# A fused attention and long-convolution kernel: one list of turns, engines and buffer slots exchanged for another

## The chip, the cores and the metric

The kernel runs on one core of a Trainium2 chip. The core has a matrix engine (TensorE, PE in the profile), a vector engine (VectorE, DVE), an activation engine (ScalarE, ACT), a general engine (GpSimd, POOL) and a sequencer that issues transfers (SyncE, SP); sixteen DMA engines move the data. Each engine works through its own list of instructions in order and waits on semaphores for the others. The metric is the time on the device in microseconds (us), the median of several executions.

## What is computed

Two independent parts stand side by side in the output. Part A is attention with a memory over segments: 2048 positions of 576 channels, 32 heads of 18 channels, four segments of 512 positions. Part B is a gated convolution: a short filter of four taps on k, a product with v, a causal convolution over the whole sequence with a filter of 2048 taps for each channel, and a product with q.

```
# part A, for each of four segments s
p     = softmax(q_s k_s^T * scale + mask)        # mask: -1e9 where row < column
a_dot = p v_s
a_mem = (phi(q_s) M) / (phi(q_s) z + 1e-6)
o     = g * a_mem + (1 - g) * a_dot
M    += phi(k_s)^T v_s ;  z += sum phi(k_s)
out_A = concat(o) @ wo
# part B
k_shift = 4-tap causal filter of k ;  kv = k_shift * v
y       = irfft(rfft(kv padded) * rfft(ssm_k padded))[:S] + kv * ssm_D
out_B   = q * y
out     = concat([out_A, out_B], axis=-1)
```

## The kernel before, in words

The program first builds a graph of 1317 operations (`Prog.build`), each of them a few instructions with the buffers it reads and writes. Nothing in the kernel decides an order at run time: three tables of numbers, `TURN`, `ENGINE` and `SLOT`, say in which order the operations are written out, on which engine each of them stands where two are possible, and which copy of a rotating buffer each logical buffer takes. `plan()` reads them, and the loop `for o in order: o.fn(o.eng)` writes the instructions. The order on an engine is therefore that of `TURN`, and all transfers are issued by SyncE in that order, one behind the other: a transfer whose data is not ready holds up all that stand behind it.

```
    order, eng, slot = ints(TURN, "H"), ints(ENGINE, "B"), ints(SLOT, "B")
    for b, k in zip(bufs, slot, strict=True):
        b.slot = k
    return pr, [ops[i] for i in order]
```

The names used below, with the lines of their instructions:

- Part A, segment s (0 to 3): the transposing loads of x, five tiles `xT` (L737, "x1" is segment 1); the products with wq and wk on TensorE (L136, out in PSUM), their casts to `dn` (L142 on ScalarE, L144 on VectorE), the stores of `dn` to a scratch in memory (L768, "qd") and the padded loads of four heads from it (L778, "pad s.hg"). For each group of four heads, 32 groups in all (numbered 0 to 31): scores on TensorE (L966, "s0", "s1", "s2"), exps on ScalarE (L973, two of 128x1024 for each score block), masks on GpSimd (L980), the product with V (L138, "av"), its copy `ou` and the store of it to a second scratch (L1026, "ad"). From that scratch the sums (L1040, "cs") and the numerators (L1068, "am") of a segment are read back, divided (L1046, L1047, L1074), joined with the memory part (L1083, and L804, L810 for phi) and multiplied with wo ("out", L136); the output leaves at L1104 ("oA").
- Part B, five groups of channels (0 to 4, the last one half as wide): the transposing loads of k (L389, "kT") and v (L392, "vT"), the four-tap filter as products with diagonal matrices (L136, "conv") and the product with v on VectorE (L422), the store of it (L428, "kvst"). The long convolution is a chain of small products: "F1" (L138, reads `xs`, loaded at L455 as xsh from the filter or xsx from kv; 512 KB), "F2", products on VectorE (L525 and following), "inv" into `Z`, a transposing transfer of `Z` to `CT` (L558, "zt"), "last" (L138, reads `CT`), the product with q (L585) and the store (L592, "yo").
- Constants: tables of sines on ScalarE (L274, L276, L322), which need the sine set of ScalarE's function tables, while L643, L804 and L973 need the exp set; copies and casts need neither. An ACT_TABLE_LOAD stands wherever the set changes.

Buffers rotate over few copies: five tiles `xT` (so x of the next segment waits until the last product with this segment's x is done), three `pad`, four `X` for k and v, one `Z` and one `CT`.

Of the kernel before, what the change touches and what calls it, by code (L numbers as in the profile page):

```python
# [1159 lines left out]

ENGS = ("PE", "ACT", "DVE", "POOL", "SP")
TURN = (
    "AwBqAAAAVABnAFUAAgABAGgAawBpAFMACABWAAQAbwBZAGwAHABXAGQAWABtAHAAWgBbAGYAngAFAGMAnQCaAAkACgALAG4ADACbAHEAZQCfAB8AiQAeAIwAIQAgAA0AmAB7AIgAlwCcAA4AHQB8AI"
    "sAoQCNAJkAIgClAA8ABwCKAKAAdQB2AKYAowCBACMApAAQAHcAeQBeAKIAeACRACQAkgCTAHoAJQCAACYAlQB+AKkAJwCqAJQAsAAoALIAlgAZACkADwQsAKsAfwCxAHIArAARAF8AtAAaACoAtQBz"
    "ABAEtgC4ABcEdAARBLkAjgC6ABUEYQCzAI8APQEYBBMEPgEUAIIAFgQSBBUAtwAUBJAAuwC8ABcAvQA7ARIAPAETAD8BGACnAKgAGQQiBCoEvwAjBMEAKwQtAK0AwAB7AcMAKwB6AcQArgB8ARYAMg"
    "QzBMIAxQBAAcoAQQHLABoEQgHMAMYAIARcASEEGwTHAB4EvgAfBMgAfQAuAM4AXQHPAC8AMgDQAEsEMAAcBB0EgwDSAF4BhAAxAGAB1AAkBNMAMwBEAdkAQwHRACUE2gAmBBsAXwGFAE8BYADJAM0A"
    "3QDbAEwERQHVAN8A3gCYATQAUAHWACcEYgHkAJkBNQDXAOYAKATlANwA6AApBOAA4QDpADoE6gDiADsELAQdAS0E7ADuAGUBNARGAS4ENQTnAGMBLwRkAUcB2ABIAeMAVQTtAPcAMATrADYEZgH4AD"
    "EEIAH5AO8AGAFnAfAASgHxAPMA9ABoAUkBNwRRBGEBhgBNBEsB9QBTBFIENwBPBE4EVARDBDwE+gD2AIcAUAT7APwAPQQZAWkBcQE4BDkAOQRiAAIBHAFqAR8BawEeAUQENgAEATgAUQFcAGwBVQEh"
    "Af0ABgFtAQMBCAHyAAcBOwA6ADwAPgQNAa8AcgEPAQ4BbwFdAAUBPwRNAUwBPQD+AP8AQAQ+AE4BQQQAAREBEwFzAQkBEAFcBIcEWASaAVMBXQQSAZsBAQFZBAoBtAFUAQsBnAG2AZ0BUgEUAVYEbg"
    "FBAEIEtQEVAXcBgQGAAXABFgF+AX0BQAAGAD8AVwQXAXgBeQG3AYIBdQGtAYMBdAF/Aa8BdgGEAa4BDAGgAYUBNQKwAVoEngGhAaUBhgFbBIcBNgKfAaYBQgCnAagBNwKpAUMARQAjARoBRACrAUYA"  # L1170
    "qgG4AboBrAFHBEcAOAIbAUUEsQEpAbkBRgQoAWAEsgFhBCIBuwGIAVcBJgEqASUBJAFWAUgAJwG8AWgEvQFYAaIBSARpBMcByQE0AcgBiQGPATkCMwFLADUBowGKAbMBvwHKAYsBwAGQATABNgGRBM"
    "EBLwGMAb4BkQHOAdABXgQxAW4EXwRvBGYElQHPAUkAdgRnBHUCKwF3BGoELAF0AmIELQHSAWsEYwRsBMIB1AF2Ao0B0QFkBG0EWQHTAcMBiASOAZYBxAFlBMUB1QHWAUoAlwGSAVAAxgFNANcBLgHY"
    "Ad0BTABPAE4A3wHLAd4BcATMAVEAcQSTAZQBOwLZAc0BeATbAToC2gF5BDwCDQI+AkkE4QFaAuAB3AFyBHoEPQJzBFYCPwLiARICdATjAQ4CWQJ7BFcCNwHkAewBdQRYAloB7gFKAhECOAFbAeUB7Q"
    "FdAkkCOQFcAuYBEwIWApICkwJbAvMBFQJ8BF4C7wH1AUoEjwT0AYsEfQRfAhcClAKQBGAClQJDAugBRAKMBOoB6QHrAWECRQJ+BGsC+wFoAv0BRgLwAfwB8QH3AfYBRwKNBGwC+QH4AecBbQJ/BGkC"
    "TAKJBI4ESAJvAvIBlgSKBEEC+gGXBG4CcAICAkACAwL+AZoCagIEAv8BBgKABJsCQgIAAsMEYgKYApkCgwQFAmUCGgJjAggCkgRPAgcCmAROAgkCcQJkAoEEkwTEBHIClASCBJkEUAJzAgoClgKVBJ"
    "cCdwILAmYCeAJ5AoQEpwJnAn4CAQKpAlIAqAJ7AnoCpAE6AUsCfAIMAqMCGAJ9AoACfwKGBKoCpQKfAh4CIgKkAqECoAKcAg8CnASBAp0EpASaBDIDnQIvA6YCMwObBKICogSrAqMEpQSuAhACsAId"
    "AqwCrwKqBBkCMQOrBBsCHwIhArECMAMUArIEggIjAiACxQSzBJ4EHAJRAjQDsgLGBJ8ENQO0ArMCwQKtAsMCMgFNAiQCwgK1Ai0CLgI2A8QCLwKPArkCtgKQAlEDUwIlAoYCQwMwAiYCugKmBIUEuw"
    "K9ArcChwKRAr8CJwKgBIgCyAJSAr4CKgLJAoMCoQQpAsoCzAK4ArwCKwLNAsACywJQA8UChAKMAs4CNwPNBMYChQLXAo0CiQLZAtgCUgNVAo4COAPbAjkDzwLcAtACOwPdAscC0wKKAtECiwJUAzoD"
    "DAPVAtQC5gLeAtICVAI8A9oCaAPoAqcEaQPiAucC5AJEAywCagPWAgcD4wLfAuACqATpAu0C7wLlAjEC4QJTA6kEMgIIAw8D7gIQA6wECwOtBLQEMwJXA/ACRQNVAw0DrgTqAusCVgM+A7UE9QIRA/"
    "YCtgT3Aj0DtwTxAhIDuATzAuwCPwO8BK8EuwTyAlgDAANIAwEDsAT4ArkE/AL0AgID+QJJA7EEQQP9Av4C+gKBA4MDAwNAA/8CfQNCA4IDBAP7AmMDWgOeAmIDXANZA38DYAMFAxQDXQNmA34DZQNe"  # L1180
    "A18DDgNkA1sDZwOMA44DawMoAmEDkAONA5IDugQGA70EkQNsAxgDCQPLBL4EvwQKA8cEzATABMkEyATQBG0DygQcAzQC0QTUBEoD0gTTBBsD1QQXA84EbgMZA4ADEwNxA5MD1gQdAxUDzwTeBIUD1w"
    "TCBN8EFgMeAxoD2ASGAycDKAOEAyMDRwP/BCQDhwMpA4gD2QRyA28D2gTBBIkDJQNzA4oDSwObA3ADKgMmA0wD2wR6A5wDjwOdA+AEdwOUA9wERgOVA90ElgOqA+EE6ASrA+YEKwPpBOIEiwMsA6wD"
    "5wR7A3gDnwP4BOMEfAMtA6ADeQMfA6ED6gTrBCADpgOoA60DpwPkBCEDogOXA5gDAAXwBHQDmQPlBJ4DqQOaA+4ErgPvBK8D8QS1A6MDdQPyBKQDdgO2A+wD7ARNA7cDAQXtBMAD8wTBA7gDAgX3BP"
    "QEBQWwA8IDxAPGA6UDCAXFAwMF9QQJBQYFuQPDA+UDBAUKBfADugPHA7sDBwW8AwwF5gMWBRQFDQULBesD7QPvA/EDFQXIAxcFsQPuA8kDGAX2BE4DTwP5BLID+wSzA7QDywPKAxkF+gT8BL0DvgPN"
    "A8wD0wPVAyIDGgUOBQ8F3gPUA98DGwUSBf0E2gMTBf4E4AO/AxAF3APnA+ED1gPbA88DIAXOAy4D0APRAxEFHwUcBd0DHQXiA/QD0gPXA/ID6APjA+QD8wPYA9kDHgX1AyEF9gPpA/wD6gMiBfcD+A"
    "MkBfkD+wP6A/0D/gMABP8DAQQCBAQEAwQHBAUEBgQIBAwECQQLBA0EIwUKBA4E")
# [81 lines left out]
```

## Time and profile before

| | |
|---|---|
| median of 3 runs | 342.2 us (341.65 to 343.16) |
| the profiled execution | 346.51 us, its span 344.8 us |
| busy over the span | PE 270.6 us (78%), ACT 247.3 (72%), DVE 244.9 (71%), POOL 105.8 (31%) |
| DMA, queue of SyncE | 51.99 MB in 132142 packets, 71.7% of sixteen engines' time |
| mean granted clock of TensorE | 0.931 |

The span is the time from the first to the last instruction; 1.7 us lie around it. No engine is busy all the time. Busy shares are averages over the whole program: what sets the pace is read for each stretch by itself, from which wait ends last there.

### The profile page before, as it was taken

What the parts mean: (1) busy time and instruction counts of PE and PEld (TensorE: products, weight loads), DVE (VectorE), ACT (ScalarE), POOL (GpSimd) and SP (SyncE); (2) the same over time, 40 slices, a digit from 0 to 9 for tenths busy, and PEclk for the clock granted to TensorE, in tenths of its full rate; (3) what the DMA queues carried; (4) which work ended last, traced back from release to release, by engine and by line L of the source; (5) the groups of instructions that cost most, each with busy time, mean ns of one, the idle gap of its engine ahead of it and who ended that gap; (6) DMA issues with size and microseconds to landing.
All of it is one profiled execution on the core that took longest, in us unless ns stands there. A gap on an engine that the chain in (4) does not pass through costs nothing.

```text
span 344.8 us, 9276 instructions
## 1 busy us (share of the span) xinstructions
PE 270.6 (78%) x3850; PEld 167.3 (49%) x3855; DVE 244.9 (71%) x400; ACT 247.3 (72%) x290; POOL 105.8 (31%) x150
## 2 busy tenths in 40 slices
...
GB/s 138 279 115 155 191 130 155 196 110 163 193 182 195 188 153 212 155 205 60 164 192 130 248 92 163 197 171 92 135 165 132 130 165 120 95 177 80 139 57 84
DMA packets 132184, 52.58 MB, mean 152 GB/s; under 512 B 112430, under 2 KB 124910, under 8 KB 132142
## 3 DMA queue, kind: packets, MB, share of 16 engines
q1 hardware_dynamic: 132142, 51.99, 71.7%
...
## 4 chain that ended last, share of the span: by engine, by line
PE 30%; DMA 20%; ACT 18%; DVE 15%; SPq 12%; issue 5%; POOL 0%; DVEq 0%; ACTq 0%
PE PS L136 18%; ACT P L973 14%; PE PS L138 8%; DMA am<-a_scratch 5%; SPq L737 5%; DMA pad<-qk_scratch 5%; PE PS L966 3%; DMA CT<-Z 3%; DMA a_scratch<-ou 2%; DMA X<-in_B_v_dram 2%; DMA skb<-in_B_shift_k_dram 2%; DVE am L1074 2%; DVE dn L144 1%; ACT A L142 1%; DVE xs L315 1%
## 5 line engine op out<-in xcount | busy, mean ns | idle before, releaser
L973 ACT ACTIVATE P<-PS 128x1024 bf16<-128x1024 f32 x160 | 154.2, 1035 | 43.6 <-PE PS L966 33.4
L980 POOL TENSOR_SCALAR_AFFINE_SELECT P<-P 128x512 bf16<-128x512 bf16 (+1 forms) x112 | 79.5, 725 | 199.1 <-ACT P L973 116.8
L966 PE MATMUL PS<-pad 18*128 18x128 bf16 (+3 forms) x512 | 35.9, 314 | 12.5 <-DMA pad<-qk_scratch 5.7
L136 PE MATMUL PS<-xT,wq 128*126 128x512 bf16 (+1 forms) x100 | 28.4, 415 | 11.6 <-DMA xT<-in_A_x_dram 11.1
L966 PEld LDWEIGHTS <-pad 18*128 18x128 bf16 x512 | 11.2, 93 | 36.2 <-issue 26.8
L136 PE MATMUL PS<-wo,am 126*128 126x288 bf16 (+1 forms) x160 | 26.7, 322 | 2.4 <-DVE am L1083 1.1
L136 PE MATMUL PS<-X,dg 128*128 128x512 bf16 x75 | 21.6, 416 | 7.6 <-DMA X<-in_B_k_dram 6.3
L138 PE MATMUL PS<-P,V 128*32 128x256 bf16 (+3 forms) x512 | 23.8, 307 | 4.4 <-ACT P L973 1.6
L136 PE MATMUL PS<-xT,wk 128*126 128x512 bf16 (+1 forms) x100 | 26.6, 400 | 0.5 <-DMA wk<-in_A_wk_dram 0.4
L144 DVE CAST dn<-PS 126x1024 bf16<-126x1024 f32 (+1 forms) x16 | 19.5, 1219 | 9.4 <-ACT P L973 4.4
L138 PE MATMUL PS<-G,PQ 64*128 64x128 bf16 (+1 forms) x640 | 23.5, 225 | 3.3 <-ACT P L973 1.7
L138 PEld LDWEIGHTS <-Ft 128*64 128x64 bf16 x704 | 21.2, 114 | 7.2 <-issue 6.4
L138 PEld LDWEIGHTS <-PQ 64*128 64x128 bf16 (+1 forms) x640 | 20.5, 102 | 8.4 <-issue 7.0
L136 PE MATMUL PS<-wv,xT 128*128 128x288 bf16 x160 | 22.6, 291 | 2.2 <-ACT V L142 1.5
L138 PE MATMUL PS<-A,Ft 128*64 128x128 bf16 (+1 forms) x640 | 22.6, 223 | 2.0 <-ACT P L973 1.0
L138 PE MATMUL PS<-W,xs 128*64 128x128 bf16 x576 | 20.9, 220 | 4.1 <-ACT P L973 2.3
L136 PEld LDWEIGHTS <-wq 128*126 128x126 bf16 (+1 forms) x100 | 13.3, 141 | 21.2 <-issue 9.4
L144 DVE CAST A<-PS 128x1024 bf16<-128x1024 f32 x18 | 21.6, 1217 | 2.7 <-PE PS L138 2.6
L422 DVE TENSOR_TENSOR X<-PS,X 128x1024 bf16<-128x1024 f32 x10 | 12.1, 1222 | 15.7 <-PE PS L136 14.2
L138 PEld LDWEIGHTS <-xs 128*64 128x64 bf16 x576 | 17.9, 109 | 9.0 <-issue 7.8
L136 PEld LDWEIGHTS <-am 126*128 126x128 bf16 (+1 forms) x160 | 16.8, 109 | 11.2 <-issue 3.0
L804 ACT ACTIVATE fe<-dn 126x512 bf16<-126x512 bf16 (+1 forms) x30 | 19.1, 639 | 2.4 <-DVE fk L810 1.9
...
## 6 DMA issues: line engine op xcount, KB each, us to landing
...
```

The costliest lines, as they stand in the source:

```text
L136: self.nc.tensor.matmul(out, lhsT=lhsT, rhs=rhs, start=start, stop=stop)
L138: self.nc.tensor.matmul(out, lhsT=lhsT, rhs=rhs, start=start, stop=stop, tile_position=pos)
L142: self.nc.scalar.copy(out=out, in_=in_)
L144: self.nc.vector.tensor_copy(out=out, in_=in_)
L315: v.tensor_scalar(out=self.i32(ix), in0=self.i32(it), scalar1=self.t(self.bcol)[:, 0:1], scalar2=self.t(off)[:, 0:1], op0=ALU.mult, op1=AL ...
L422: self.nc.vector.tensor_tensor(out=self.t(kv)[:, sl], in0=self.psf(pc), in1=self.t(vT)[:, sl], op=ALU.mult)
L737: self.nc.sync.dma_start_transpose(out=self.t(b)[:], in_=self.A_x[0, L * s:L * s + L, c0:c0 + P])
L804: self.nc.scalar.activation(out=self.t(fe)[0:M], in_=self.t(dense[m])[0:M, w_, :], func=ACT.Exp)
L966: nc.tensor.matmul(o, lhsT=t[r, 1, q0:q0 + P], rhs=t[r, 0, q0:L], start=True, stop=True, tile_position=(32 * j, 0))
L973: self.nc.scalar.activation(out=out2(jj), in_=self.psf(pso[jj]), func=ACT.Exp, scale=scale)
L980: self.nc.gpsimd.affine_select(out=ap, in_=ap, compare_op=ALU.is_ge, fill=0.0, base=0, pattern=pat + [[1, P]], channel_multiplier=-1)
L1074: self.nc.vector.tensor_tensor(out=self.t(b)[0:M], in0=self.psf(pR)[0:M], in1=self.t(b)[0:M], op=ALU.mult)
```

## The change

Only the three tables are different. The operations, their instructions, shapes and buffers are the same; the turns are others on every engine and in the transfer queue, and some casts and evictions that either ScalarE or VectorE can do, and some sums that VectorE or GpSimd can do, stand on the other engine (ScalarE has 283 operations instead of 282, VectorE 308 instead of 309). The diff is three long strings; the first line of each:

```
 TURN = (
-    "AwBqAAAAVABnAFUAAgABAGgAawBpAFMACABWAAQAbwBZAGwAHABXAGQAWABtAHAAWgBbAGYAngAFAGMAnQCaAAkACgALAG4ADACbAHEAZQCfAB8AiQAeAIwAIQAgAA0AmAB7AIgAlwCcAA4AHQB8AI"
...
+    "AwBoAFYAAABrAAEAWAACABwACABXAFMAagBpAGcAVQBUAAQAHgAdAG0ABQAJAAoAWwAfAGwAbwBuAAsAcABxAGQAWQCJABQAWgCIAIsAZQAMAA0AXgBmABUAEgCMABMADgAgAJcAigCNAHsAmACaAJ"
...
```

Three places of the new order follow. The first is SyncE's queue in the first third, around the first transfer of `Z` to `CT` (zt0). The names are X4 for the rotating k and v tiles, qk_scratch and a_scratch for the two scratches. Before:

```order
L428 DMA kv_scratch_171<-X4_0_99 128x2048
L455 DMA xs_1_104<-in_B_ssm_k_dram 128x32x64
L768 DMA qk_scratch_172<-dn_1_120 4x18x1024
L778 DMA pad_2_130<-qk_scratch_172 128x1024
L768 DMA qk_scratch_172<-dn_0_119 7x18x1024
L558 DMA_TRANSPOSE CT_0_98<-Z_0_101 128x32x128
L392 DMA_TRANSPOSE X4_1_100<-in_B_v_dram 128x2048
L389 DMA_TRANSPOSE X4_0_99<-in_B_k_dram 128x2048
L1026 DMA a_scratch_173<-ou_1_158 128x512
```

Now:

```order
L455 DMA xs_1_104<-kv_scratch_171 128x32x64
L392 DMA_TRANSPOSE X4_1_100<-in_B_v_dram 128x2048
L778 DMA pad_0_128<-qk_scratch_172 128x1024
L778 DMA pad_2_130<-qk_scratch_172 128x1024
L428 DMA kv_scratch_171<-X4_0_99 128x2048
L558 DMA_TRANSPOSE CT_0_98<-Z_0_101 128x32x128
L1026 DMA a_scratch_173<-ou_1_158 128x512
L1026 DMA a_scratch_173<-ou_0_157 128x512
L389 DMA_TRANSPOSE X4_0_99<-in_B_k_dram 128x2048
```

The load of the third filter group (xs from in_B_ssm_k) and two stores to qk_scratch are gone from between the store of kv and zt0; the load of v stands ahead of zt0, that of k two rows behind it.

The second place is ScalarE at the start. W1, psc and Ft are the sine tables, fe an exp of phi, gg two exps of the gate, G and dn and V and phk casts, P4 the exps of the scores. Before:

```order
L804 ACT_TABLE_LOAD
L804 ACTIVATE fe_1_166<-dn_0_119 126x512
L804 ACTIVATE fe_0_165<-dn_1_120 126x512
L142 CAST V_1_132<-PS_63 128x32x18
L322 ACT_TABLE_LOAD
L322 ACTIVATE Ft_79<-xs_0_103 128x16x64
L142 CAST dn_0_119<-PS_63 126x1024
L142 CAST V_3_134<-PS_63 128x32x18
L804 ACT_TABLE_LOAD
L804 ACTIVATE fe_0_165<-dn_0_119 126x512
```

Now:

```order
L804 ACT_TABLE_LOAD
L804 ACTIVATE fe_1_166<-dn_1_120 126x512
L322 ACT_TABLE_LOAD
L322 ACTIVATE Ft_79<-xs_0_103 128x16x64
L142 CAST G_80<-PS_63 128x1024
L804 ACT_TABLE_LOAD
L804 ACTIVATE fe_0_165<-dn_0_119 126x512
L142 CAST G_80<-PS_63 128x1024
L322 ACT_TABLE_LOAD
L322 ACTIVATE Ft_79<-xs_0_103 128x16x64
```

The sines and the exps alternate oftener: the whole list of ScalarE has 8 ACT_TABLE_LOAD where it had 6, all of them in the first part. The loads of x for segment 1 wait on the last product of segment 0 that reads x; it is the 29th operation of TensorE's list before and the 32nd now.

The third place is SyncE's queue near the end, where the transfer of Z for the fourth group (zt3) and the last pads stand. Before:

```order
L1040 DMA cs_0_167<-a_scratch_173 64x1x128
L1068 DMA am_5_147<-a_scratch_173 126x1x512
L558 DMA_TRANSPOSE CT_0_98<-Z_0_101 128x32x128
L778 DMA pad_2_130<-qk_scratch_172 128x1024
L778 DMA pad_1_129<-qk_scratch_172 128x1024
L1026 DMA a_scratch_173<-ou_0_157 128x512
```

Now:

```order
L778 DMA pad_1_129<-qk_scratch_172 128x1024
L1026 DMA a_scratch_173<-ou_1_158 128x512
L778 DMA pad_2_130<-qk_scratch_172 128x1024
L558 DMA_TRANSPOSE CT_0_98<-Z_0_101 128x32x64
L1040 DMA cs_1_168<-a_scratch_173 64x1x128
L1026 DMA a_scratch_173<-ou_0_157 128x512
```

zt3 stands 16 rows ahead of the second pad now and no longer right before the two; the transfer in the last fence is the fifth one (zt4), half as large, which stood between the last stores of ou (L1026) and the last sums (L1040) before.

## Rows read from the trace of the kernel before

**Rows 1.** Busy time by stretch: start:end, length, then each engine, clock, DMA, GB/s.
```profile
0.00:45.00 45.00, 28.40 (x190) 15.95 (x192) 26.65 (x60) 24.85 (x31) 18.51 (x30) 0.96 0.81 174
98.00:130.00 32.00, 22.55 (x274) 12.73 (x274) 20.53 (x38) 18.27 (x23) 7.47 (x10) 0.89 0.93 184
255.00:300.00 45.00, 35.51 (x716) 25.38 (x713) 35.08 (x46) 35.54 (x41) 14.16 (x19) 0.92 0.58 131
300.00:322.00 22.00, 16.37 (x335) 10.94 (x327) 13.98 (x20) 17.89 (x21) 6.63 (x9) 0.77 0.59 136
322.00:345.00 23.00, 10.10 (x52) 5.97 (x52) 6.47 (x10) 2.30 (x4) 0.00 (x0) 0.70 0.35 84
```

**Rows 2.** Waits of PE from 45 to 345 us: total, times, longest.
```profile
PE PS L138 <- DMA CT<-Z: 10.1, 2, 7.4
PE PS L136 <- DMA X<-in_B_k_dram: 6.3, 1, 6.3
PE PS L136 <- DMA xT<-in_A_x_dram: 1.8, 1, 1.8
```

**Rows 3.** Timeline of PE, 97 to 131 us: start, length, engine, line, instruction.
```profile
115.67 1.29 PE L136 MATMUL PS<-fq,zm 126*128 126x128 bf16 x20
123.25 0.59 PE L136 MATMUL PS<-X,dg 128*128 128x512 bf16 x1 [6.28 <-DMA X<-in_B_k_dram]
```

**Rows 4.** Timeline of SyncE's queue (SPq), 100 to 131 us.
```profile
102.47 0.34 SPq L428 DMA_DIRECT2D kv_scratch<-X  x1
102.85 0.42 SPq L455 DMA_DIRECT2D xs<-in_B_ssm_k_dram  x1
103.60 3.16 SPq L768 DMA_DIRECT2D qk_scratch<-dn  x1
...
107.31 1.34 SPq L768 DMA_DIRECT2D qk_scratch<-dn  x1
108.76 7.32 SPq L558 DMA_TRANSPOSE CT<-Z  x1
116.12 2.68 SPq L392 DMA_TRANSPOSE X<-in_B_v_dram  x1
118.89 2.21 SPq L389 DMA_TRANSPOSE X<-in_B_k_dram  x1
```

**Rows 5.** Issues of the transposes of Z: ns min/median/max, first and last start.
```profile
L558 SPq DMA_TRANSPOSE CT<-Z x5: 3084/5356/7315, 108.8 to 323.7; - x5
```

**Rows 6.** The same for the stores to qk_scratch (L768).
```profile
L768 SPq DMA_DIRECT2D qk_scratch<-dn x20: 666/775/3157, 18.7 to 276.5; - x20
```

**Rows 7.** Timeline of ACT, 30 to 46 us.
```profile
36.23 1.94 ACT L973 ACTIVATE P<-PS 128x1024 bf16<-128x1024 f32 x2 [0.48 <-PE PS L966]
38.18 1.28 ACT L322 ACT_TABLE_LOAD   x1
39.48 1.06 ACT L322 ACTIVATE Ft<-xs 128x1024 bf16<-128x1024 int32 x1
```

**Rows 8.** Timeline of SyncE's queue, 295 to 345 us.
```profile
298.05 5.36 SPq L558 DMA_TRANSPOSE CT<-Z  x1
303.51 0.98 SPq L778 DMA_DIRECT2D pad<-qk_scratch  x2
...
311.76 1.32 SPq L1026 DMA_DIRECT2D a_scratch<-ou  x1
316.60 0.74 SPq L1040 DMA_DIRECT2D cs<-a_scratch  x1
...
321.92 1.69 SPq L1026 DMA_DIRECT2D a_scratch<-ou  x2
323.65 3.08 SPq L558 DMA_TRANSPOSE CT<-Z  x1
326.85 1.24 SPq L1040 DMA_DIRECT2D cs<-a_scratch  x1
```

**Rows 9.** Timeline of ACT, 290 to 345 us.
```profile
309.35 3.77 ACT L973 ACTIVATE P<-PS 128x1024 bf16<-128x1024 f32 x4 [3.26 <-PE PS L966]
313.83 5.80 ACT L973 ACTIVATE P<-PS 128x1024 bf16<-128x1024 f32 x6 [0.71 <-PE PS L966]
319.49 1.92 ACT L142 CAST Z<-PS 64x1024 bf16<-64x1024 f32 x2
```

More of the change, by code (lines that the diff above doesn't have):

```diff
@@ new lines @@
+    "AwBoAFYAAABrAAEAWAACABwACABXAFMAagBpAGcAVQBUAAQAHgAdAG0ABQAJAAoAWwAfAGwAbwBuAAsAcABxAGQAWQCJABQAWgCIAIsAZQAMAA0AXgBmABUAEgCMABMADgAgAJcAigCNAHsAmACaAJ"
+    "sADwCdAJwAEACeABYApQCfAF8AIwB2AKYAmQB1ABEAfAAhAIAAdwAPBCIAcgCjAJIAcwCkALAAdACOAJEAoQCyAH0AoACTALEABwCiAI8AqQB+ABAEqgAZAJAAgQAXABoApwC0ALMAqAC1ABgAEwQR"
+    "BCUAFAQkABIEtgCCAHkAYwC3ACYAeABcALgAegA7ASgAPQEVBLoAFgS5ABcEYgAnADwBYACVABgElAC/ACkAwQC7AMAAvADDAJYAxADCAKsAvQCsACIEPwEjBMUArQA+AYMAygCuACoEKwQyBMYAyw"
+    "DMADoExwB9ASoAyAAzBDsEzgB/AAYAvgDNAF0A0AB+AX8BzwBAASsA0gBBAdQAQgHZABkE0wDaAF8BQwHVANsA3QCFAN8ARAHRAC0A3gCEABwERQFcAckAhgAaBNwAHgQgBBsEHQRgAR8E1gAhBOAA"
@@ new lines @@
+    "FQUfA20DDQUgAyEDjwOTA5sDnQMrA/YELAOcA54DlwOUAw4FLQNuA5gDcQMPBZ8DlQOZA28DcANyA4sD+wShA5oDIgP5BKADcwMuA6ID+gRNAxAFJwMRBUwD/AQoA6YDowMpAyQDdwN0A5YDpAMjA/"
+    "4EdQN2A6cD/QSoA6oDeAMlAxIFqwN5A6wDsQMWBRMFsgOpA7MDFwUYBbkDrQO7A3oDrgO6A7UDewO0A7cDGQWvA3wDtgOlAxwFwAPCA08DGgW8A8EDHQUbBbADxAPFA7gDxgO9A74DwwNOA8cDHgXP"
+    "A9oD0QPIA9sD0APlA9wD3QPTA9UD0gPJA78D1APLA9YD5gPsA80DygPMA94DJgPgA+sDHwXOAyAF7QPnA+8DKgPoA/AD1wPfA/ED8gPhA+ID2APuAyEF8wMiBfQD2QPjA+QD9QPpA/gD/APqA/YD+w"
+    "P9A/cD/gP5A/oDAAT/AwQEIwUBBAMEAgQFBAYEJAUHBAgEDAQLBAkECgQNBA4E")
```

81 lines of the change are left out of this document (37 added, 44 removed).

## The prediction

> **What bounds the kernel now.** I read the shares by engine first, then the busy time by stretch, the waits of TensorE, the timelines around the longest waits, and SyncE's queue there. The shares say that no engine bounds the whole: TensorE, ScalarE and VectorE are each busy for 71 to 78% of the span. By stretch [rows 1] TensorE is idle for 45 - 28.40 = 16.6 us of the first 45, for 9.45 us from 98 to 130, for 9.5 us from 255 to 300, 5.6 from 300 to 322 and 12.9 in the last 23. These five stretches hold 54 us of its idle time; between them it is nearly full and its own work sets the pace. So what the order of turns can change is what TensorE waits for in these five, and whether new waits appear between them.
>
> Its waits name transfers [rows 2]: 10.1 us for `CT`, the transposed Z, in two waits of 7.4 and 2.7; 6.3 us in one wait for k; 1.8 us for x. The one for k stands behind the 20 products of the memory's denominator, which end at 116.96, and lasts to 123.25 [rows 3]. Why k is late is read from SyncE's queue [rows 4]: the store of kv at 102.47, the load of the third filter group (xs, 512 KB), two stores to qk_scratch, then zt0, whose issue alone takes 7.32 us, then v, and k as the last at 118.89. The issue of a transfer lengthens when those ahead of it are not drained: a store to qk_scratch takes 3.16 us there, its median is 0.775 [rows 6]; zt0 takes 7.32, the median of the five is 5.356 [rows 5].
>
> At the end zt3 takes 5.36 us and the last two pads stand behind it [rows 8], and ScalarE then waits 3.26 us for the scores that need them [rows 9]. After the last exps (at 319.49 ScalarE goes over to Z) come the last stores of ou, zt4, the last sums, and the tail to 344.8.
>
> **The change part by part.** The sum is made against the profiled execution, 346.51 us with 344.8 us of span; the median of the runs shown is 342.2, so a time on its scale is multiplied by 342.2/346.51 = 0.9876 for the forecast.
>
> *The start: +3.0.* ScalarE gets two table loads more, of 1.28 us each [rows 7]: 2.57 us. They stand in its list ahead of the first exps, so nothing on ScalarE itself hides them; what can hide them is that it is idle for 45 - 24.85 = 20.15 us of that stretch anyway [rows 1], which gives a lower end of 0. The loads of x for segment 1 and all that stands behind them in SyncE's queue wait for a product that is three operations later; if that delay adds to the loads once more, the upper end is twice 2.57, or +5.1. I take 3.0, the loads and a little of the second, since the loads are the row nearest.
>
> A rule of the Trainium skill speaks against this part: "ScalarE: Activation LUTs", section "What ACT_TABLE_LOAD costs", puts a switch of the function set at about 2.66 us, the load and a drain of 1.38 us. The trace does not bear out the drain: a pair of exps starts at 36.23 and takes 1.94, the load starts at 38.18, and the sine at 39.48 [rows 7], so the switch is 1.30 us in all. By the rule the two switches would cost 5.3 us and the sum would be 2.7 us later, 341.1 us on the median's scale.
>
> *The wait for k: -5.0.* Between the store of kv and zt0 the load of xs and the two stores are gone [the order, first place]. What they cost is read as the excess over the medians behind xs: 3.16 - 0.775 = 2.4 us on the first store, 1.34 - 0.775 = 0.6 on the second, 7.32 - 5.36 = 2.0 on zt0, and the medians of the two stores and 0.42 of xs itself, 2.0 us; together 7.0 us [rows 4 to 6]. Two things take some of it back: two stores of ou stand between zt0 and k, and v stands ahead of zt0 now, where it must wait until the four-tap filter of the third group has left its buffer. I allow 2 us for both, the length of v's 2.68 less a part of it that is covered by TensorE's own work. That leaves 5.0. The ends are -6.3, the whole wait, and 0, if zt0 itself, which still stands ahead of k, is what keeps k late.
>
> *zt3 away from the last pads: -2.8.* The pads are no longer behind its 5.36 us; the wait of ScalarE for the scores is 3.26 [rows 9]. Most of it goes. Next late is TensorE's own work for these scores, which costs the rest. Ends: -3.3 and 0.
>
> *The tail: -1.0.* zt4 (3.08) leaves the place between the last stores of ou and the last sums. But the sums read what these stores write: with the store issued at 311.76, the sums came at 316.60, 4.84 us later; with the stores of 321.92 they came at 326.85, 4.93 later [rows 8]. So zt4 lies beside the landing and hides nearly whole. What goes is the longer issue of the sums behind it, 1.24 against 0.74, and the two casts of Z (1.92, of which the masks behind the last exps cover the greater part) [rows 8, 9]. Ends: -2.5 and 0.
>
> *New waits between the stretches: +2.0.* Three transposing loads now stand in SyncE's queue right behind a store that needs a late result: k of the fifth group behind a store of ou, two of the five x of segment 3 behind a store of oA, and zt2 behind another store of oA. I price them at one wait like that for x, 1.8 us [rows 2]. Ends: 0, and 6.3, a wait like that for k.
>
> All other moves I cost at nothing: the same instructions are covered by the same neighbours where TensorE is full. Where a move takes the cover away, it shows as a wait of TensorE of about 0.5 us, as there are many now.
>
> Sum: +3.0 - 5.0 - 2.8 - 1.0 + 2.0 = -3.8 us. 346.51 - 3.8 = 342.7, times 0.9876 is 338.4 us.
>
> **The rivals.** *A denser end (faster).* From 255 to 322 ScalarE is idle for 9.46 + 4.11 = 13.6 us [rows 1]. The change puts the convolution's work of the fourth group well ahead of this place, so that exps are left with little else between them. If ScalarE is idle for only 5 us there, this term is -8.6 in place of -2.8: -9.6 in all, 336.9, or 332.7 us. For it: exps that follow each other take 0.97 each without a gap [rows 7, 9]. Against it: their scores still wait for pads, and the clock granted to TensorE is 0.92 and 0.77 there [rows 1], lower when it has less to do.
>
> *k is late as before (no change).* zt0 still stands ahead of k. If its 7.32 us are the transpose's own and not the backlog's, the term for k is 0: +3.0 + 0 - 2.8 - 1.0 + 2.0 = +1.2, 347.7, or 343.4 us. For it: other zt's take 5 us and more with less ahead of them [rows 5]. Against it: the store ahead of it was slow too [rows 4].
>
> *The queue's head waits (slower).* The three loads behind late stores: SyncE stands still until an eviction is done, and x, k and `CT` come late one after the other. At 3.4 us each, between the 2.7 of the shorter wait for `CT` and the 6.3 for k [rows 2], they cost 10.2 in place of 2.0: +4.4 in all, 350.9, or 346.5 us. It decides the sign from 5.8 us of such waits on. For it: SyncE's queue is what TensorE's longest waits go back to now. Against it: TensorE has other work in its list between the store's source and the load's user.
>
> *A switch of table sets at twice its load*, by the gaps on ScalarE, would give 341.1 us; the rows show none such, and I count it in with no change at 0.02.
>
> **How the numbers follow.** Forecast 0.40, denser end 0.18, k late as before 0.15 (with the 0.02), the queue's head 0.27. The time is that of the forecast, 338.4 us; its own range, with the ends of the terms taken half, is 335 to 342. The range of 8 in 10 reaches half way past the two outer cases: 330.5 to 347. A measurement of this kernel can tell about 0.5%, 1.7 us, from no change. Faster than 340.5: 0.37 of the forecast's 0.40 and the denser end, 0.55; slower than 343.9: 0.27 for the queue's head; the rest, 0.18, is the same.
>
> **What would show it.** Right: the first exps come no more than 3 us later than 36.2; eight table loads of 1.28 us; TensorE's wait for k is under 2 us; ScalarE has no gap of 3 us in its last 40 us; no single wait for x, k or `CT` above 2.5 us in the middle. Wrong: the first scores of the next groups fall 5 us and more behind, k still ends a wait of 5 us, or new waits for `CT`, x or k stand between 130 and 260 us. If ScalarE's last exps follow without gaps from some 280 us on, the end is denser than I take it.

## The result and the profile after

The changed kernel takes 333.84 us (median of 4, 329.13 to 337.65) beside 342.68 us for the kernel before (341.65 to 343.94) on the same chip; the ratio is 0.9659, with a 95% interval of 0.9546 to 0.9772. It is taken over undisturbed executions alone and so lies below the ratio of the two medians, 0.974. On another chip it took 334.63 beside 343.88. It is faster by some 9 us, where 3.8 were forecast: the sign and the range of 330.5 to 347 held, but the forecast's own range of 335 to 342 did not, the size was more than twice the forecast, and the rival called the denser end, 332.7 us, came closer.

The profiled execution took 334.69 us with a span of 333.0, against 346.51 and 344.8: 11.8 us of span less. The profiled execution of the kernel before is longer than its median by 3.8 us, so differences between these two traces come out somewhat larger than those of the medians. The busy time by stretch of the changed kernel (columns as in [rows 1], the last two stretches cut at the end of its last exp):

```profile
0.00:45.00 45.00, 25.27 (x213) 16.32 (x214) 20.56 (x57) 29.60 (x35) 12.40 (x26) 0.96 0.72 168
45.00:98.00 53.00, 46.26 (x682) 27.10 (x681) 46.65 (x74) 44.48 (x54) 25.05 (x33) 1.00 0.92 173
98.00:130.00 32.00, 26.66 (x343) 15.97 (x342) 21.03 (x37) 22.93 (x29) 7.24 (x10) 0.89 0.83 170
130.00:200.00 70.00, 61.44 (x914) 39.54 (x911) 61.03 (x97) 52.40 (x64) 15.94 (x21) 0.98 0.85 170
200.00:256.00 56.00, 51.23 (x845) 33.25 (x841) 45.64 (x70) 50.69 (x56) 20.10 (x27) 1.00 0.69 156
256.00:310.10 54.10, 43.05 (x791) 27.45 (x795) 38.35 (x55) 48.51 (x54) 23.27 (x31) 0.93 0.64 148
```

The kernel before in the stretches that [rows 1] does not have in this cut:

```profile
45.00:98.00 53.00, 46.40 (x742) 28.29 (x739) 44.24 (x73) 43.02 (x51) 16.02 (x27) 0.97 0.89 156
130.00:200.00 70.00, 63.02 (x942) 40.10 (x942) 59.00 (x100) 56.67 (x68) 18.68 (x27) 1.00 0.75 168
200.00:256.00 56.00, 49.26 (x653) 28.79 (x647) 39.66 (x60) 49.43 (x58) 24.31 (x30) 0.97 0.67 147
256.00:319.70 63.70, 49.11 (x989) 34.34 (x990) 47.66 (x64) 50.45 (x58) 19.55 (x26) 0.87 0.57 130
```

ScalarE does all the exps, so its last exp is a good place to cut: before it ends at 313.83 + 5.80 = 319.63 us [rows 9], now at 310.05. Up to there ScalarE is busy for 248.61 us instead of 242.69 (+5.9, of which two more table loads are 2.6), and idle (length less the fourth engine's figure) by so much less or more: -4.75 in the first 45 us (its busy time there is 4.75 longer), -1.5 to 98, -4.7 to 130, +4.3 to 200, -1.3 to 256, and -7.7 from there to the last exp (63.70 - 50.45 = 13.25 before, 54.10 - 48.51 = 5.59 now). Together -15.5 + 5.9 = -9.6. The rest comes behind the last exp: 344.8 - 319.63 = 25.2 us before, 333.0 - 310.05 = 22.95 now, -2.2. What the stretch of k gives (-4.7) is given back in the next one (+4.3); what stays is the end. Counted by exps it is the same: in the traces the 111th of the 160 starts at 244.7 us, 11 us later than before (233.7), the 141st at 291.3 beside 291.5, the last at 308.9 instead of 318.6. The new order puts exps off, does work of the convolution in their place, and gains among the last twenty.

The waits of TensorE from 45 us on (total, times, longest), to be laid beside [rows 2]:

```profile
PE PS L138 <- ACT P L973: 6.2, 17, 0.6
PE PS L136 <- DVE rs L1047: 5.7, 3, 3.7
PE PS L966 <- DMA pad<-qk_scratch: 4.2, 1, 4.2
...
PE PS L136 <- DMA X<-in_B_k_dram: 0.6, 1, 0.6
```

The kernel before has two more waits among its first four, which [rows 2] does not show:

```profile
PE PS L138 <- ACT P L973: 8.5, 18, 2.3
PE PS L966 <- DMA pad<-qk_scratch: 5.7, 4, 2.6
```

The waits for `CT` and for x are gone, that for k is 0.6. What leads now, short waits for exps, is not new. Pads were waited for before as well, four times; the one wait of 4.2 us that is left is explained by SyncE's queue (start, length, line, transfer):

```profile
99.54 5.81 SPq L392 DMA_TRANSPOSE X<-in_B_v_dram  x1
105.39 1.72 SPq L778 DMA_DIRECT2D pad<-qk_scratch  x2
107.21 0.38 SPq L428 DMA_DIRECT2D kv_scratch<-X  x1
107.69 6.27 SPq L558 DMA_TRANSPOSE CT<-Z  x1
...
115.16 2.36 SPq L389 DMA_TRANSPOSE X<-in_B_k_dram  x1
```

k is issued only 3.7 us earlier than in [rows 4], behind a zt0 that still takes 6.27. TensorE no longer waits for it because other products stand in its list first: its products with k begin at 124.55. The price of having v ahead is the late pads. It follows the length of v's issue, which differs from execution to execution of the same order: 5.81 us and a wait of 4.2 here, 3.63 and 2.0 in the second profile below, 2.34 and no wait in the run with four exps twice.

At the end, ScalarE (start, length, instruction and count, wait before it):

```profile
289.50 7.44 ACT L973 ACTIVATE P<-PS 128x1024 bf16<-128x1024 f32 x8
297.11 12.94 ACT L973 ACTIVATE P<-PS 128x1024 bf16<-128x1024 f32 x14 [0.17 <-PE PS L966]
```

Twenty-two exps follow each other in 20.55 us with one wait of 0.17 us, where [rows 9] has 3.26 and 0.71 among its last ten. In the kernel before the last twenty-two take 31.3 us, from 288.33 on, and the waits are the smaller part of that: eight casts of ScalarE stand between them, 7.8 us, six of them the convolution's. Three lines of them (`A`, `Hx` and `PQ` are the fifth group's):

```profile
297.93 1.10 ACT L142 CAST A<-PS 128x1024 bf16<-128x1024 f32 x1
...
300.66 2.03 ACT L142 CAST Hx<-PS 128x1024 bf16<-128x1024 f32 x2
302.56 1.05 ACT L142 CAST PQ<-PS 128x1024 bf16<-128x1024 f32 x1
```

Now none stands there: six of the eight are done by VectorE, two earlier on ScalarE. And the tail of the queue:

```profile
299.42 3.04 SPq L558 DMA_TRANSPOSE CT<-Z  x1
...
311.95 1.94 SPq L1026 DMA_DIRECT2D a_scratch<-ou  x2
...
315.49 0.69 SPq L1040 DMA_DIRECT2D cs<-a_scratch  x1
```

zt4 is 16 us ahead of the last sums, which come 3.54 us after the start of the stores that they read, instead of 4.93.

The granted clock is not the cause. A second profile of the changed kernel (span 332.4) has nearly the mean granted clock of the kernel before, 0.933 beside 0.931, and TensorE as long busy as before, 270.6 us; the first line of its page's busy times:

```profile
PE 270.5 (81%) x3855; PEld 168.6 (51%) x3855; DVE 240.8 (72%) x399; ACT 252.4 (76%) x293; POOL 105.4 (32%) x150
```

Its idle time is 332.4 - 270.5 = 61.9 us, against 344.8 - 270.6 = 74.2 before.

### The profile page after: what moved, and what is told of

The parts are those of the page before. It is cut to its first block, busy times and chain, and to the rows that moved or that the text cites. A ratio compares the mean times of both kernels' runs of the same rounds, so it can differ in the third digit from the quotient of the medians.

```text
span 333.0 us, 9289 instructions
## 1 busy us (share of the span) xinstructions
PE 265.6 (80%) x3855; PEld 166.7 (50%) x3855; DVE 241.5 (73%) x399; ACT 252.3 (76%) x293; POOL 105.2 (32%) x150
## 4 chain that ended last, share of the span: by engine, by line
PE 37%; ACT 21%; DVE 17%; DMA 15%; issue 5%; SPq 4%; POOL 0%; DVEq 0%; ACTq 0%
PE PS L136 20%; PE PS L138 13%; ACT P L973 13%; DMA a_scratch<-ou 5%; PE PS L966 4%; DMA am<-a_scratch 3%; DMA cs<-a_scratch 2%; DMA X<-in_B_v_dram 2%; SPq L737 2%; DVE Hx L144 2%; DVE A L144 2%; DVE dn L144 1%; DVE PQ L525 1%; DMA wq<-in_A_wq_dram 1%; DVE am L1074 1%
## 5 line engine op out<-in xcount | busy, mean ns | idle before, releaser
L973 ACT ACTIVATE P<-PS 128x1024 bf16<-128x1024 f32 x160 | 153.3, 1033 | 25.3 <-PE PS L966 17.2
L980 POOL TENSOR_SCALAR_AFFINE_SELECT P<-P 128x512 bf16<-128x512 bf16 (+1 forms) x112 | 81.1, 740 | 187.6 <-ACT P L973 147.1
L966 PEld LDWEIGHTS <-pad 18*128 18x128 bf16 x512 | 11.8, 93 | 37.6 <-issue 29.7
L138 PE MATMUL PS<-P,V 128*32 128x256 bf16 (+3 forms) x512 | 25.2, 322 | 5.1 <-ACT P L973 3.0
L136 PE MATMUL PS<-xT,wq 128*126 128x512 bf16 (+1 forms) x100 | 26.0, 399 | 1.9 <-ACT P L973 1.2
L136 PE MATMUL PS<-wo,am 126*128 126x288 bf16 (+1 forms) x160 | 24.5, 307 | 3.7 <-DVE am L1083 2.0
L136 PE MATMUL PS<-wv,xT 128*128 128x288 bf16 x160 | 24.1, 304 | 2.7 <-ACT phk L142 2.0
L136 PEld LDWEIGHTS <-wk 128*126 128x126 bf16 (+1 forms) x100 | 12.4, 135 | 20.3 <-DMA wk<-in_A_wk_dram 8.6
L138 PE MATMUL PS<-G,PQ 64*128 64x128 bf16 (+1 forms) x640 | 21.7, 220 | 1.1 <-ACT P L973 0.6
L138 PEld LDWEIGHTS <-PQ 64*128 64x128 bf16 (+1 forms) x640 | 19.0, 98 | 6.1 <-issue 4.5
L144 DVE CAST dn<-PS 126x1024 bf16<-126x1024 f32 (+1 forms) x11 | 13.4, 1220 | 10.9 <-PE PS L136 8.8
L138 PEld LDWEIGHTS <-V 128*32 128x32 bf16 x512 | 11.6, 100 | 18.0 <-ACT P L973 5.1
L142 ACT CAST A<-PS 128x1024 bf16<-128x1024 f32 x19 | 18.8, 1026 | 2.4 <-PE PS L138 2.2
```

The lines of the kernel that those rows point to most:

```text
L136: self.nc.tensor.matmul(out, lhsT=lhsT, rhs=rhs, start=start, stop=stop)
L138: self.nc.tensor.matmul(out, lhsT=lhsT, rhs=rhs, start=start, stop=stop, tile_position=pos)
L142: self.nc.scalar.copy(out=out, in_=in_)
L144: self.nc.vector.tensor_copy(out=out, in_=in_)
L966: nc.tensor.matmul(o, lhsT=t[r, 1, q0:q0 + P], rhs=t[r, 0, q0:L], start=True, stop=True, tile_position=(32 * j, 0))
L973: self.nc.scalar.activation(out=out2(jj), in_=self.psf(pso[jj]), func=ACT.Exp, scale=scale)
```

## The experiments

The question behind all of them: is the gain the forecast's own sum (k, the pads, the tail), or a denser end? Each expectation names its own two theories. All ratios are to the kernel before, run beside on the same chip. One thing no run separates: of the 1317 operations 97 stand on another engine in the changed kernel (46 go from VectorE to ScalarE and 45 the other way, 3 and 3 between VectorE and GpSimd), and the buffer slots are others too. The two halves below take their engines and slots along, the other runs move turns alone.

**The changed kernel again.** No edit.

> The changed kernel once more, as the base for the edits beside it. Theory A (the gain is a denser end: ScalarE idle for 5.6 us from 254 to its last exp, where it was idle for 13.2 us over the same work, and a full granted clock there): 0.965 to 0.975 of the kernel before, the last exp some 10 us earlier than before. Rival B (the gain is mostly one disturbed profile, and the change is worth what the forecast said): 0.985 to 0.99.

334.63 us (median of 6), 0.973 of the 343.88 beside it. The last exp ends at 309.62 us. Theory A's time and its last exp hold (this ratio is of medians, without an interval); of its two grounds, ScalarE is idle for 7.0 us from 254 us to that exp instead of 5.6, and the granted clock there is 0.91, not full.

**Half of the order each.** The first 700 of the 1317 operations in one order, the rest in the other; buffer slots follow.

```diff
 ab185:  order = new[:700] + (old without these)
 ba185:  order = old[:700] + (new without these)
```

> The first 700 operations as in the changed kernel (to some 183 us), the rest in the order of the kernel before. Theory A, the gain lies in the end: 0.99 of the kernel before, since the trace of the changed kernel is 3.3 us ahead at the cut (182.3 against 185.6 us), and the old end's gaps (13 us of idle ScalarE between 258 and 322) are back. Rival B, the wait for k carries the gain: 0.975 or less, most of the changed kernel's gain, and the gaps of the end are smaller although its order is the old one.

> The mirror: the first 700 operations as in the kernel before (to some 186 us), the rest in the new order. Theory A: 0.975 of the kernel before, ScalarE idle for under 7 us in the 55 us before its last exp, the wait of TensorE for k at 123 us as long as before (6 us). Rival B: 0.99 or above.

ab185: 343.55 us, 0.9994 (0.9945 to 1.0044). ba185: 344.61, 1.000 (0.9952 to 1.0048). Neither half alone gives anything: theory A's 0.99 and 0.975 both failed, and B's 0.975 for ab185 as well; only B's 0.99 or above for ba185 fits. In both the seam costs: of some 13 operations each half expects done what the other has left to it (in ba185 TensorE waits 2.29 us for phi at 185.57, in ab185 2.34 at 168.28, 1.52 at 183.35 and 1.65 at 185.64). In ba185 TensorE also waits 6.4 us for k, as theory A said, and its last twenty-two exps take 20.55 us, as in the changed kernel. The traces tell the halves apart by two instructions that all have: the issue of the sums of segment 1 (L1040, around 198 us), and the fourth of the forty last products with wo. In the new order that one begins the last long run of products; in the old one it stands by itself. In the changed kernel, in ba185 and in the kernel before, the queue (where shown) and TensorE:

```profile
197.81 0.58 SPq L1040 DMA_DIRECT2D cs<-a_scratch  x1
```
```profile
322.64 6.78 PE L136 MATMUL PS<-wo,am 126*128 126x288 bf16 x37 [2.02 <-DVE am L1083]
```
```profile
203.93 0.57 SPq L1040 DMA_DIRECT2D cs<-a_scratch  x1
```
```profile
328.88 6.68 PE L136 MATMUL PS<-wo,am 126*128 126x288 bf16 x37 [2.14 <-DVE am L1083]
```
```profile
333.63 0.42 PE L136 MATMUL PS<-wo,am 126*128 126x288 bf16 x1 [0.45 <-DVE am L1083]
```

| execution | end in the order | sums at | product at | between |
|---|---|---|---|---|
| before | old | 198.53 | 333.63 | 135.1 |
| k alone (below) | old | 198.75 | 332.38 | 133.6 |
| ab185 | old | 197.65 | 329.16 | 131.5 |
| after | new | 197.81 | 322.64 | 124.8 |
| after again | new | 196.08 | 322.00 | 125.9 |
| ba185 | new | 203.93 | 328.88 | 125.0 |

Whatever stands ahead, the second part takes 125 to 126 us in the new order and 131 to 135 in the old: 8 us on average, nearly the whole gain. ba185 has the whole wait for k in its first part, starts its second 6 us late by its seam and keeps that. (Its profiled execution, 340.86 us, is its shortest; its median shows less of this than the trace.)

**k alone.** The load of k moved in the queue of the kernel before.

```diff
 L428 DMA kv_scratch<-X_0_99 128x2048
+L389 DMA_TRANSPOSE X_0_99<-in_B_k_dram 128x2048
 L455 DMA xs_104<-in_B_ssm_k_dram 128x32x64
...
 L558 DMA_TRANSPOSE CT_98<-Z_101 128x32x128
 L392 DMA_TRANSPOSE X_1_100<-in_B_v_dram 128x2048
-L389 DMA_TRANSPOSE X_0_99<-in_B_k_dram 128x2048
```

> The kernel before with one transfer moved: the transposing load of k (kT3) stands right behind the store of kv, ahead of the filter's load, the two stores to qk_scratch and zt0, instead of behind them all. Theory A (the forecast's term for k is right by itself): TensorE's wait of 6.3 us at 123 us goes and 5 us with it, 0.985 of the kernel before. Rival B (the time is only lent: what stands behind k in the queue, and the later groups, comes as late as before): the wait goes, the time stays within 0.5%.

345.17 us, 1.0049 (1.0014 to 1.0083): rival B, at its edge. The wait for k is gone, and two others have come; TensorE, and the queue:

```profile
126.02 0.61 PE L966 MATMUL PS<-pad 18*128 18x384 bf16 x8 [3.05 <-DVE X L422]
132.51 0.58 PE L136 MATMUL PS<-rs,selb 128*72 128x128 bf16 x4 [2.84 <-DVE rs L1047]
```
```profile
111.99 7.75 SPq L558 DMA_TRANSPOSE CT<-Z  x1
119.79 2.85 SPq L392 DMA_TRANSPOSE X<-in_B_v_dram  x1
```

Now v is the last behind zt0, and VectorE's product of k and v waits for it.

**The two late transposes alone.** zt3 behind the last pads and zt4 behind the last sums in the kernel before, their products and stores following.

```diff
-L558 DMA_TRANSPOSE CT_98<-Z_101 128x32x128
 L778 DMA pad_130<-qk_scratch 128x1024
 L778 DMA pad_129<-qk_scratch 128x1024
+L558 DMA_TRANSPOSE CT_98<-Z_101 128x32x128
...
-L558 DMA_TRANSPOSE CT_98<-Z_101 128x32x64
 L1040 DMA cs_167<-a_scratch 32x1x128
 L1068 DMA am_143<-a_scratch 72x1x512
 L1068 DMA am_145<-a_scratch 126x1x512
+L558 DMA_TRANSPOSE CT_98<-Z_101 128x32x64
```

> The kernel before with its two late transposes of Z moved in the queue: zt3 behind the last two pads instead of ahead of them, and zt4 behind the last sums and numerators; the products that read them (last3 behind two scores, last4 ahead of the last product with wo) and their stores follow. Theory A (the forecast's third and fourth terms, -2.8 and -1.0): ScalarE's gap of 3.26 us at 309 us is gone or under 1 us, 0.989 of the kernel before. Rival B (the gap closes, but the scores behind it wait for their exps' buffers or for TensorE at half clock, and the tail waits for the stores of ou): 0.996 to 1.0.

347.49 us, 1.0125 (1.0089 to 1.0161): slower than either theory said. ScalarE's gap at 309 us is gone and stands 5 us on, larger:

```profile
306.71 3.91 ACT L973 ACTIVATE P<-PS 128x1024 bf16<-128x1024 f32 x4 [0.76 <-POOL P L980]
314.84 5.82 ACT L973 ACTIVATE P<-PS 128x1024 bf16<-128x1024 f32 x6 [4.22 <-PE PS L966]
```

There the scores stand behind inv of the fifth group in TensorE's list (inv starts at 312.34, after 1.60 us of waiting for VectorE's product with q, which reads the products with `CT` that the edit moved there). The gap belongs to the convolution between the exps, not to one transfer. The tail is longer too: from the last exp to the end 26.5 us instead of 25.2, since TensorE waits 4.05 us for the `CT` of the late zt4 behind the sums. The edit takes both transposes out of the way by moving them back, where the changed kernel has them further ahead; that way of doing it was not tried by itself.

**Four exps twice, in both kernels.** This adds the second pass to scores 0 and 1 of group 29:

```diff
-    self.nc.scalar.activation(out=out2(jj), in_=self.psf(pso[jj]), func=ACT.Exp, scale=scale)
+    for _ in range(2 if nm in ("s0_29", "s1_29") else 1):
+        self.nc.scalar.activation(out=out2(jj), in_=self.psf(pso[jj]), func=ACT.Exp, scale=scale)
```

> The changed kernel with four of the last exps done twice (scores 0 and 1 of group 29, the same input and output again): 4 x 0.93 = 3.7 us more work for ScalarE in its dense last stretch, nothing else. Theory A (ScalarE sets the pace of the new end): 3.3 to 3.7 us more, 1.010 to 1.011 of the changed kernel, 0.98 of the kernel before. Rival B (TensorE or the queue sets it): under 1.5 us more.

> The same four exps done twice in the kernel before. Theory A (the old end was set by TensorE's list and the transposes, with ScalarE waiting 3.26 us at 309 us right behind): the gap takes up 2.5 to 3.3 of the 3.7 us, 1.00 to 1.004 of the kernel before. Rival B (ScalarE set the old end as well): 1.010.

The changed kernel: 336.91 us, 0.9824 (0.9776 to 0.9873). The ratio is theory A's 0.98; but it is 2.3 us over the 334.63 on the other chip, short of A's 3.3, so the time does not settle it. In the trace the dense stretch is longer by all of the added work (the added line makes L974 of L973):

```profile
286.65 7.44 ACT L974 ACTIVATE P<-PS 128x1024 bf16<-128x1024 f32 x8
294.95 17.15 ACT L974 ACTIVATE P<-PS 128x1024 bf16<-128x1024 f32 x18 [0.86 <-POOL P L981]
```

286.65 to 312.10 is 25.45 us, 289.50 to 310.05 was 20.55: the four exps, 3.7, and 1.2 of waits. This execution came to the stretch 2.9 us earlier than the changed kernel's, so its last exp ends only 2.1 us later. The kernel before: 347.05 us, 1.0084 (1.005 to 1.0117): theory A's time failed here, and rival B's 1.010 lies in the interval. The gap of 3.26 did close, to 0.54, as A had it; but the exps behind it still start 3.3 us later (312.68 instead of 309.35), because the delay had grown to 6 us by then (the exps ahead of the gap start at 310.20 instead of 304.15). TensorE, then ScalarE:

```profile
299.23 0.64 PE L138 MATMUL PS<-W,xs 128*64 128x128 bf16 x16 [1.58 <-ACT P L974]
...
309.72 0.40 PE L966 MATMUL PS<-pad 18*128 18x512 bf16 x4 [0.72 <-ACT PQ L142]
```
```profile
307.74 1.01 ACT L142 CAST Hx<-PS 128x1024 bf16<-128x1024 f32 x1 [0.96 <-PE PS L138]
...
312.68 3.77 ACT L974 ACTIVATE P<-PS 128x1024 bf16<-128x1024 f32 x4 [0.54 <-PE PS L966]
```

So the old end was a ring: exps hold up TensorE's small products of the fifth group (1.58 us), these hold up ScalarE's casts (0.96), and the casts the next scores (0.72).

**The fifth group put back.** In the changed kernel only the fifth group's operations stand where the kernel before has them, counted by the others ahead of each:

```diff
 TensorE, operations in order
-... s2_28 av27 s1_28 num3.4 inv4.3 s0_29 inv4.2 s1_29 av28 s1_30 ...
+... s2_28 av27 s1_28 F1x4.1 num3.4 F1h4.1 F1x4.0 F2h4.0 s0_29 F2x4.0 F2x4.1 F2h4.1 s1_29 av28 s1_30 ...
```

> The changed kernel with one part undone: the operations of the convolution's fifth group (F1, F2, products, inv, zt4, last4, their casts, q and yo) stand as far down among the others as in the kernel before, between the last exps instead of ahead of them; all other operations keep the new order. Theory A (the new end is dense because the convolution's chain of TensorE, ScalarE and VectorE is through before the last exps, so that these wait for nothing else): ScalarE has gaps of 5 us and more again among the last 17 pairs of exps, 4 to 8 us more than the changed kernel, 0.985 to 0.997 of the kernel before. Rival B (the place of this group among the exps is of no weight; what counts is that TensorE comes to 255 us with less work left): under 2 us more.

356.63 us, 1.031 (1.0232 to 1.0387): the direction of theory A, with nearly three times its size. ScalarE waits again among the last exps:

```profile
303.87 1.02 ACT L973 ACTIVATE P<-PS 128x1024 bf16<-128x1024 f32 x1 [2.31 <-PE PS L966]
...
309.57 1.94 ACT L973 ACTIVATE P<-PS 128x1024 bf16<-128x1024 f32 x2 [1.93 <-PE PS L966]
...
324.58 1.02 ACT L973 ACTIVATE P<-PS 128x1024 bf16<-128x1024 f32 x1 [3.79 <-PE PS L966]
```

and TensorE for the group's casts:

```profile
294.95 0.62 PE L966 MATMUL PS<-pad 18*128 18x256 bf16 x8 [3.25 <-ACT A L142]
```

From 256 us to its last exp ScalarE is idle for 23.8 us, and the granted clock there is 0.73 instead of 0.93. 22 us over the changed kernel (on another chip) is more than the whole gain, so it does not measure what this group's place is worth: the order around it was written for its absence. It shows that the dense end needs it, and that casts on the other engine alone do not make that end: this run keeps them where the changed kernel has them.

**The table loads, the pads, the tail.** Three edits of the changed kernel that the forecast's other steps suggest, and two of them together.

```diff
 a_tab, ScalarE
 L142 CAST dn_120<-PS 126x1024
+L322 ACTIVATE Ft<-xs_103 128x16x64
 L804 ACT_TABLE_LOAD
 L804 ACTIVATE fe_166<-dn_120 126x512
-L322 ACT_TABLE_LOAD
-L322 ACTIVATE Ft<-xs_103 128x16x64
...
 a_pads, SyncE
+L778 DMA pad_128<-qk_scratch 128x1024
+L778 DMA pad_130<-qk_scratch 128x1024
 L392 DMA_TRANSPOSE X_1_100<-in_B_v_dram 128x2048
-L778 DMA pad_128<-qk_scratch 128x1024
-L778 DMA pad_130<-qk_scratch 128x1024
...
 a_warm, the last product of the convolution (behind R3.2 now) and the first with wo
-for i in range(2):
+for i in [0, 1] * (4 if gi == 4 else 1):
+for m in [0, 1, 2] * (2 if (s, tt, h) == (3, 0, 1) else 0):    # ahead of the real m loop
```

> The changed kernel with its sines grouped: the second sine ahead of the first exp of phi, the third and fourth after the gate, so that ScalarE loads 4 tables in place of 8 in the first 36 us; nothing else moves but the operations that these carry along. Theory A (the start's +3.0 of the forecast is real and is passed on to the end): 3 us less than the changed kernel, 0.99 of it, the first exps of the scores at 33 to 34 us in place of 36.0. Rival B (the start is bound by the loads of x and weights and by TensorE, and what ScalarE gains is lost in the next wait): within 0.3% of the changed kernel.

> The changed kernel with two loads of pads (pad1.0, pad1.2) ahead of the load of v (vT3) in SyncE's queue, where they stood behind it: v waits there 2.8 us for its buffer and takes 5.8 us, and TensorE then waits 4.2 us for the pad at 109 us. Theory A (of the forecast's 5 us for k only a part came, because v ahead of zt0 made the pads late): the wait for the pad goes under 1 us, 2 to 4 us less. Rival B (what is freed there is lost before the end, as with k in the kernel before): within 0.4%.

> The changed kernel with TensorE kept active in the tail: the last product of the convolution stands behind R3.2 instead of ahead of it, its four matmuls are done four times, and the first three matmuls of the last product with wo twice more, all into the same place with the same result; the product with q moves behind the last sums on VectorE. Before, TensorE stands idle for 1.9, 3.7 and 2.0 us between 312 and 323 us and its last 40 products run at a granted clock of 0.5 until 326.9 us. Theory A (the clock comes back while it is active): the last products take 3.4 to 4.5 us instead of 6.8, 2 to 3 us less, 0.992 of the changed kernel. Rival B (the clock stays at 0.5, or the repeats delay the last sums): the same or up to 1 us more.

> The changed kernel with two of the edits together: the sines grouped (4 table loads in place of 8) and the two pads ahead of the load of v. In the profiled execution of the first alone TensorE was 3 to 5 us ahead from the first third on and stayed so to the end (span 326.7 us), but its other executions were no shorter than the changed kernel's. Theory A (the earlier start is passed on, and only the granted clock of single executions hid it): 0.96 of the kernel before, 328 to 331 us. Rival B (what the start and the pads free is lost to the clock or to later waits in most executions): 0.97, as the changed kernel, 333 to 335 us.

a_tab: 333.84 us, 0.9653 (0.9548 to 0.9759). The first exps come at 32.77 instead of 36.00, and in the profiled execution a lead lasts to the end (span 326.7), but the median is that of the changed kernel: rival B. That execution, 328.44 us, is the shortest of its six, and the unedited changed kernel has executions as short: 328.99 and 329.13. So its lead is not a gain of the grouped sines. a_pads: 334.39 us, 0.9695 (0.9641 to 0.9749), rival B; the wait for the pad is gone. a_both: 333.69 us, 0.9726 (0.9671 to 0.9781), rival B. a_warm: 335.58 us, 0.9692 (0.9623 to 0.976), rival B, although the clock did come back sooner. A stretch of a_warm, then one of the changed kernel (the figure behind the five engines is the granted clock):

```profile
324.00:328.00 4.00, 3.79 (x31) 2.74 (x29) 0.00 (x0) 1.28 (x2) 0.00 (x0) 1.00 0.66 139
```
```profile
320.00:326.00 6.00, 3.98 (x18) 2.20 (x17) 2.13 (x4) 0.64 (x1) 0.00 (x0) 0.50 0.04 7
```

The repeats themselves fill most of what the clock gives back: 46 products in 6.97 us, starting at 320.82, against 37 in 6.78 starting at 322.64. The last product ends 1.6 us sooner in this trace; the time does not show it. No version was measurably faster than the changed kernel.

## Why the prediction was right in sign and short in size

- **The start, +3.0: of no weight in the time.** The first exps come at 36.00 us, not later than the 36.23 before, though all eight loads now stand ahead of them and two of the six stood behind them before (one of these is in [rows 7]). TensorE is idle for 45 - 25.27 = 19.7 us of the first 45, 3.1 more than before [rows 1], and 1.6 more in the second profile; the sums of segment 1 are issued no later for it. With the loads grouped the median stays where it is (a_tab, a_both). A switch of table sets costs its load alone here too (a load at 33.71, the exp behind it at 35.00), so the rival with twice that price fell.
- **The wait for k, -5.0: right for its stretch, wrong for the end.** TensorE is idle for 5.3 instead of 9.45 us there, -4.1. Alone it brings nothing (b_k), ScalarE's idle time gives it back by 200 us, and ba185 has its fast second part with the whole wait for k ahead of it. The step reckoned zt0's 7.32 as backlog; it takes 6.27 with a short store in front.
- **zt3 and the last pads, -2.8: the step that was mis-sized.** The end is worth 7.7 us of ScalarE's idle time (6.2 in the second profile), near the 8.6 that the rival put there. Its mechanism was misread too: the scores of [rows 9] did not wait for the pads but stood in TensorE's list behind the products with `CT`, which waited for zt3. TensorE of the kernel before:

```profile
306.77 1.92 PE L138 MATMUL PS<-CT,Psi 128*64 128x512 bf16 x8 [2.72 <-DMA CT<-Z]
308.62 0.61 PE L966 MATMUL PS<-pad 18*128 18x512 bf16 x4
```

  The scores then wait for no pad. "Next late is TensorE's own work for these scores" was true of the old list; in the new one the convolution's work ahead of them is done before. The rival's ground against itself, a lower clock in the end, did not hold: 0.93 up to the last exp and 0.91 in the second profile, before 0.87.
- **The tail, -1.0: right in kind, -2.2 in size.** The sums come earlier behind their stores, and zt4 no longer delays them.
- **New waits, +2.0: did not come.** No wait for x or `CT` is left from 45 us on. x of the last segment is loaded later, as foreseen, but is also wanted 19 us later. The first products with it, before and after:

```profile
205.50 0.43 PE L136 MATMUL PS<-xT,wq 128*126 128x512 bf16 x1
```
```profile
224.81 1.39 PE L136 MATMUL PS<-wv,xT 128*128 128x288 bf16 x10
```

  In between TensorE has the convolution's third and fourth groups, which is what empties the end. The step looked at the queue and not at TensorE's list, and the rival of the queue's head fell with it.

The sign was in part luck. Three of the five terms (+3.0, -5.0, +2.0) did not reach the end, and they happen to add up to nothing; the -3.8 that is left is the two terms of the end, which had the right place and less than half the size.

Shown is: nearly the whole gain lies behind 198 us; there the last exps run without a gap and without casts between them; the two moves of the old order that were tried do not bring it; and it goes when the fifth group is put back. Open is how the 9 us divide among the groups brought forward, and what part the 97 operations on other engines (six of the eight casts that left the end among them) and the other buffer slots have in it.
